# Output projection of a gated attention kernel over 448 instead of 512 rows: the last four heads' rows moved into padding rows, the rest as pairs of 64-row tiles

## The chip, the core and the metric

The kernel runs on one core of one Trainium2 chip. Its engines work side by side, each from its own list of instructions in order: TensorE (PE in the profile, its weight loads PEld), VectorE (DVE), ScalarE (ACT), GpSimd (POOL) and SyncE (SP), which here only issues DMAs. The time is the device time of one launch in microseconds (us). PE multiplies a stationary tile of up to 128 rows (the contraction) by 128 columns with a stream of up to 512 columns and adds into PSUM, which has 8 banks here of 128 x 512 f32.

## The reference

Two branches share the input x of 2048 tokens by 448 features and are mixed by a gate of one value per token.

```
g = sigmoid((x * gate_w).sum(-1))
a = A(x):  q, k, v = x @ wq, x @ wk, x @ wv         # 16 heads of 28
           4 segments of 512 tokens; in each, per head
             a_dot = softmax(q k^T / sqrt(28) + causal mask) v
             a_mem = phi(q) M / (phi(q) z + 1e-6)    # M, z: sums over earlier segments
             o = sigmoid(beta) * a_mem + (1 - sigmoid(beta)) * a_dot
           a = o @ wo                                # 448 x 448: the output projection
b = B(x):  an MLP over the token axis: layernorm, w1 (2048 x 1792), gelu, w2 (1792 x 2048)
out = g * a + (1 - g) * b
```

The change concerns `o @ wo`: for each of 16 tiles of 128 tokens, a contraction over the 448 rows (16 heads of 28).

## The kernel before

**Heads and padding.** Attention wants the heads at multiples of 32 rows. `qT` (128 rows, 4 head groups, 2048 tokens; L428 on, reused as `oT` for the attention's output) holds four heads in each group: head l at rows 32 l to 32 l + 27, and four padding rows behind it. So 448 rows of `o` lie in 4 x 128 = 512 rows. `wo_sb` (128 rows, 4 groups, 448 columns) holds wo in the same layout. `load_wo` brings it by four DMAs, and `pool_clears` sets it to zero beforehand with one memset on POOL, so that the padding rows count for nothing. `wo_tile(T)` makes one tile of 128 tokens: four full matmuls, one for each head group, into one PSUM bank, and then an evacuation `ag`, which may be on ACT or DVE, that applies the gate and adds the MLP's bias.

**Order.** `Sched` collects operations with what they read and write, and works out the waits. The order on every engine isn't worked out: it is written by name in the table `ORDER`, five lists, together with the PSUM bank that an operation takes (`wo12=7` takes bank 7). Banks 4 to 7 are shared by projections, attention, output projection and MLP; an operation that takes a bank waits for those that read its last content. SP issues its DMAs in the order of its list, and a DMA that has to wait for something keeps back those behind it.

**Names.** u is a matmul of the MLP's first layer, y of its second (`y9-3`: tile 9, fourth matmul); `ldw1_k` and `ldw2_k` load their weights into three slots, in turn, so that a load waits until the tiles that used the slot three loads ago are done. k, q and v with letters are the projections. `sc` are the scores, `exp` the exponentials on ACT, `pv` the product with v, `mem` the memory part, `mst` the memory's state. On DVE `ta` and `tm` transpose pv's and mem's results from PSUM, `eps`, `rec`, `oa`, `om` normalize, `o` on POOL adds the two, and `ot` transposes the sum back into `oT`; unit u has segment u // 4 and head group u % 4, so ot15 is the last. `fin` adds the MLP's part and `out` stores a tile. `gk`, `gq`: the last heads' rows of k and q go by DMA to DRAM (`spare_heads`) and back to the place where attention wants them. `tk` and `dtx` are DMA transposes.

**Tile shapes on PE.** Full matmuls have 128 rows and 128 columns. The scores use 28 of 32 rows, four heads side by side (L973). `pv` and `mst` use 32 columns, four side by side (L1011, L858). The projections have pairs of 64 rows (L711). `Sched.columns` turns a short run of full matmuls next to a `pv` or `mst` into four column tiles each (L286 instead of L284).

Of the kernel before, what the change touches and what calls it, by code (L numbers as in the profile page):

```python
# [7 lines left out]
BF16 = mybir.dt.bfloat16  # L8
# [3 lines left out]
S = 2048  # L12
# [62 lines left out]
class Sched:  # L75
# [13 lines left out]
    def op(self, eng, fn, reads=(), writes=(), name=None, dma=False, out=False, cost=100.0, prio=0.0, mode=None,  # L89
           nbytes=0, rel=0.0, port=False, take=None, use=(), alt=None, split=None):  # L90
# [24 lines left out]
        if dma:  # L115
            self._dma_uid += 1
            o.evspace = "dma_u%d" % self._dma_uid
            o.is_event = True
# [183 lines left out]
def pool_cost(n):  # L302
# [7 lines left out]
        warm fill0 fill1 fill2 trx1_0=4 trx1_1=5 trx0_0=6 fill3 gtr trx0_1=7 fill4 fill5 v03t v03s v03a v03b v03c  # L310
        k0a=45 v03d k0c k0b=67 q0a k0d q0b q0d q0c v67a=54 sc0_0 v67c k1a=67 k1c sc0_1 k1b=45 k1d q1a=67 sc0_2 q1c
        q1b=45 q1d sc0_3 u0-0=6 u1-0:2=7 u0-1:2 u1-2:2 pv0=4 u0-3 sc0_4 u1-4 u0-4 u1-5 btr=5 u2-0=4 u1-6 u0-5:2 u2-1:2
        u1-7 u3-0=5 u0-7 u3-1 sc1_0 u3-2:2 u2-3 u0-8:2 u2-4 u0-10 u1-8:2 u3-4 u1-10 sc1_1 u0-11 u1-11 u3-5 u1-12
        u0-12:2 u1-13 u0-14 u1-14 u0-15 u2-5 u1-15 u2-6:2 u3-6 u2-8 u3-7:2 sc1_2 u3-9 u5-0=6 u2-9 u3-10:2 u2-10:2 u5-1
        pv1=7 sc1_3 u5-2 u2-12 u5-3 u2-13 u4-0=7 u5-4 u4-1:5 u3-12 u4-6 u2-14:2 u4-7 u5-5 sc1_4 u4-8 u3-13 u4-9 u5-6
        u3-14:2 u5-7:2 u6-0=4 u5-9 u4-10:2 u6-1 u4-12:2 u6-2 u4-14 sc2_0 u7-0=5 u5-10 u4-15 u5-11 u7-1:2 u6-3:2 u7-3
        u5-12:2 u7-4 sc2_1 u7-5 u5-14 u7-6:3 pv2=7 u5-15 u6-5 u7-9 u6-6:3 u7-10 sc2_2 u6-9 mst0=7 u6-10:2 pv3=6 u7-11
        u6-12 u7-12 sc2_3 u7-13 u8-0:2=7 u7-14 u9-0=6 u6-13 u9-1:2 u6-14 u8-2 u7-15 u8-3 sc2_4 u6-15 u8-4 u9-3 u8-5
        u9-4 u8-6:2 u9-5 pv4=5 u9-6 sc3_0 u9-7 u8-8:2 u9-8 u8-10 mem4=4 u9-9 u8-11 u9-10:4 u8-12:2 u9-14:2 u8-14:2
        k2a=45 sc3_1 k2c k2b=67 k2d sc3_2 q2a=54 q2b=67 q2c q2d sc3_3 v96a=45 v96b=67 v96c v96d sc3_4 u11-0:4=4 mem6=5  # L320
        u10-0:3=7 u11-4 u10-3 pv6=6 u10-4 u11-5 pv5=5 sc4_0 u10-5:3 u13-0=5 u10-8 u11-6:2 u10-9 u13-1 mem5=6 u11-8
        u10-10 sc4_1 u10-11:2 u11-9 u10-13 u13-2 u10-14 u11-10 u13-3 u10-15 u11-11:3 u13-4 u11-14:2 u13-5 sc4_2
        u12-0:6=6 pv7=7 u12-6 u13-6 u12-7 sc4_3 mst1=4 u12-8 u13-7:2 mem7=7 u13-9 u12-9 u13-10 u12-10 sc4_4 u13-11
        u12-11 u13-12 u12-12:3 wo2=4 u12-15 wo3=7 u13-13:3 wo0~2=4 wo1=7 sc5_0 k3a=64 k3b=57 k3c k3d sc5_1 v14a=46
        pv8=5 v14c pv9=7 wo5=5 mem9=4 sc5_2 q3a=76 q3b=54 q3c q3d sc5_3 y0-0:5=7 y1-0:2=6 y0-5 y3-0:2=4 y1-2 y3-2:2
        mem8=5 y0-6 y1-3 y3-4 sc5_4 y3-5:2 y0-7 y3-7 y0-8:2 y1-4:2 y3-8:2 y0-10 sc6_0 y3-10 y0-11:2 y3-11 wo4=5 y1-6
        y3-12 y1-7 y0-13 sc6_1 y1-8:2 y3-13 y1-10:2 mem11=5 wo6=7 y1-12:2 y4-0=5 sc6_2 pv11=4 y4-1:2 y2-0=6 y4-3
        y2-1:2 y4-4 pv10=4 y4-5 sc6_3 y2-3 y4-6 y2-4 y4-7:2 mem10=7 y4-9 y5-0:2=4 y2-5:2 sc6_4 y2-7 y5-2 mst2=7 y2-8:2
        y5-3:3 y2-10 y4-10 y5-6 sc7_0 y2-11 y5-7 y2-12 y6-0=7 y5-8:3 y2-13 y6-1 y4-11 y6-2 y5-11 y4-12 sc7_1 y5-12
        y4-13 y6-3 pv12=6 y5-13 wo7=5 sc7_2 y6-4:4 y7-0:4=5 y6-8 mem12=6 y6-9 y7-4:4 mem13=4 y6-10 y7-8:2 sc7_3 pv13=6  # L330
        y6-11:3 wo9=4 y7-10 sc7_4 y7-11:2 mem14=6 y7-13 wo8=4 pv14=7 wo10=6 wo11=5 pv15=4 y8-0:2=7 y9-0:2=5 y8-2
        y9-2:3 mem15=6 y8-3 y9-5:2 y8-4:4 y9-7 y8-8:2 y9-8:2 y11-0=6 y10-0:2=4 y9-10 y11-1 y10-2 y8-10:2 y9-11 y11-2
        y8-12:2 y11-3 y10-3 y9-12:2 y11-4 y10-4 y11-5:2 y10-5 y11-7:2 y10-6:2 y11-9 y10-8 y11-10:2 y10-9:2 y11-12
        y10-11 y11-13 y10-12:2 wo12=7 wo14=6 wo13=4 y13-0=5 wo15=7 y15-0=6 y13-1 y15-1 y13-2:2 y15-2 y13-4:2 y14-0:4=4
        y15-3 y13-6:2 y12-0:2=7 y14-4:3 y12-2 y15-4 y13-8 y14-7 y15-5:2 y14-8 y13-9 y12-3 y14-9:3 y12-4 y13-10 y15-7
        y14-12 y12-5 y13-11 y15-8 y13-12 y15-9:2 y13-13 y12-6:4 y14-13 y15-11 y12-10 y15-12:2 y12-11:3 y15-0~2=5
# [3 lines left out]
        ldx2 ldwv1 ldwv2 xTcp0_10 xTcp0_00 cpv0 cpv1 cpv2 gt0 gt1 cpv3 gt2 cpk0_0 ek0_0 gt3 cpk0_3 ek0_1 cpk0_2 cpv4  # L340
        cpq0_1 gt4 cpq0_3 tb exp0_0=2 gt7 gt6 cpk1_0 exp0_1=3 cpk1_2 cpq1_3 exp0_2=4 cpq1_1 exp0_3=0 cpv5 gt5 eq1_0
# [42 lines left out]
        gq2_3 ldw2_0 ldwo0 gq2_1 gk2_0 tk1_2 gq2_2 tk2_1 ldwo1 gq2_h1 gk2_1 gq2_h2 gq2_h0 ldw2_1 gk2_h1 gk3_2 gk2_h0  # L384
        tk2_0 ldw2_2 gq3_3 tk2_3 gk3_3 gq3_2 gq3_1 tk2_2 gq3_0 gk3_0 gk3_1 ldw2_3 gq3_h2 gk3_h0 out0 out1 out3 gq3_h1
        gk3_h1 gq3_h0 out2 out5 ldw2_4 ldw2_5 ldw2_6 out4 out7 out6 ldw2_7 out9 out8 out11 out10 out13 out14 out15
        out12 out15~2
    """,
}

# [860 lines left out]
```

The softmax here doesn't subtract the row's maximum and nothing guards it: scores larger than these inputs give would overflow.

## Time and profile before

| what | us |
|---|---|
| median of 5 runs (lowest, highest) | 173.49 (172.94, 174.56) |
| the profiled execution, and its span | 174.56, 172.8 |
| PE busy in the span | 166.5 |
| DVE, ACT, POOL busy | 144.4, 127.0, 68.4 |
| last matmul before the end of the attention (pv15) ends at | 145.87 |
| last ot (ot14) starts at | 154.96 |
| last output DMA issued, landed | 170.86, 172.35 |

The span runs from the first to the last instruction; the time of the execution holds 1.76 us more. Matmuls overlap: [...]what it costs in a stream is the distance to the next start. Instructions that wait, and SP's issues, don't count as busy.

### The profile page before, as it was taken

To read this page: it belongs to the slowest core of one execution; us is meant where nothing else is said; L and a number is where in the kernel's file an instruction comes from. 1 tells how busy PE (TensorE), PEld (TensorE's weight loads), DVE (VectorE), ACT (ScalarE), POOL (GpSimd) and SP (SyncE) were. 2 spreads that over 40 slices of the span, in tenths; PEclk is the share of its full clock that TensorE was granted. 3 is DMA by queue.
4 is the path that set the end of the run, shared out by engine and by line. 5 is a ranking of instruction groups with operands and counts; after the bars stand their busy time and mean duration, and the time that the engine had idled before them with its cause. 6 is when DMAs were issued, how large, how long until landed. Compare 5 with 4: busy or idle time off the path is not lost.

```text
span 172.8 us, 4764 instructions
## 1 busy us (share of the span) xinstructions
PE 166.5 (96%) x1960; PEld 80.4 (47%) x1960; DVE 144.4 (84%) x324; ACT 127.0 (73%) x154; POOL 68.4 (40%) x98
## 2 busy tenths in 40 slices
PE   7996999999999999999999999999999999999994
PEld 2544334445445444445455435444554445555553
DVE  1975999969897999999999999996998999977115
ACT  2375999998999999998999999989667876001000
POOL 8040457441554203193351561047736856150000
PEclk9999999999999999999999999999999999999999
DMA  5998996528382955579237000732820089825203
GB/s 171 262 236 252 304 292 152 104 67 233 66 239 40 148 126 154 110 215 282 56 76 223 0 4 10 208 70 52 239 87 30 0 233 292 226 81 172 67 0 106
DMA packets 49733, 24.57 MB, mean 142 GB/s; under 512 B 14240, under 2 KB 49472, under 8 KB 49712
## 3 DMA queue, kind: packets, MB, share of 16 engines
q1 hardware_dynamic: 49024, 23.70, 53.8%
q10 hardware_dynamic: 688, 0.57, 1.1%
q8 instruction: 15, 0.25, 0.6%
q14 instruction: 6, 0.05, 0.1%
HBM read 18.76 MB, written 2.36 MB: 122 GB/s over the span
## 4 chain that ended last, share of the span: by engine, by line
PE 72%; DVE 9%; ACT 7%; SPq 5%; DMA 3%; issue 2%; ACTq 0%
PE t L284 36%; PE t L711 15%; PE t L286 11%; PE t L973 6%; PE t L1011 4%; ACT t L982 3%; DMA t<-in_A_x_dram 3%; DVE t L1093 2%; SPq L536 2%; DVE t L1095 2%; ACT t L1087 1%; DVE t L1100 1%; ACT t L1098 1%; DVE t L806 1%; ACT t L815 1%
## 5 line engine op out<-in xcount | busy, mean ns | idle before, releaser
L982 ACT ACTIVATE t<-t 128x2048 bf16<-128x2048 f32 x40 | 75.1, 1878 | 8.3 <-PE t L973 8.0
L284 PE MATMUL t<-t 128*128 128x448 bf16 (+3 forms) x411 | 79.1, 347 | 0.2 <-DVE t L1100 0.2
L985 POOL TENSOR_SCALAR_AFFINE_SELECT t<-t 128x512 bf16<-128x512 bf16 x64 | 42.4, 681 | 48.3 <-ACT t L982 47.8
L284 PEld LDWEIGHTS t<-t 128*128 128x128 bf16 x411 | 37.8, 98 | 37.2 <-issue 4.4
L711 PE MATMUL t<-t 64*128 64x512 bf16 (+1 forms) x308 | 35.4, 368 | 2.0 <-DMA t<-in_A_x_dram 1.5
L286 PE MATMUL t<-t 128*32 128x448 bf16 (+1 forms) x508 | 28.7, 354 | 0.0
L1042 POOL TENSOR_TENSOR t<-t 128x448 bf16<-128x448 f32 x12 | 15.6, 1302 | 23.6 <-DVE t L1038 6.8
L711 PEld LDWEIGHTS t<-t 64*128 64x128 bf16 x308 | 15.7, 94 | 18.9 <-PE t L711 3.2
L1118 DVE SCALAR_TENSOR_TENSOR t<-t 128x448 bf16<-128x448 f32 (+2 forms) x17 | 10.6, 644 | 9.3 <-PE t L284 8.6
L1067 ACT ACTIVATE t<-t 128x448 bf16<-128x448 f32 x10 | 7.2, 725 | 13.2 <-PE t L284 11.6
L286 PEld LDWEIGHTS t<-t 128*32 128x32 bf16 x508 | 12.3, 96 | 8.9 <-issue 1.9
L973 PE MATMUL t<-t 28*128 28x512 bf16 (+3 forms) x256 | 15.8, 301 | 0.3
L1048 DVE STREAM_TRANSPOSE t<-t 128x512 bf16<-128x512 bf16 x16 | 10.9, 692 | 1.1 <-POOL t L1042 1.1
L916 DVE BATCH_NORM_STATS2 t<-t 128x6 f32<-128x448 bf16 x16 | 9.3, 606 | 2.8 <-DMA t<-in_A_x_dram 2.8
L1011 PE MATMUL t<-t 128*32 128x512 bf16 (+3 forms) x256 | 11.5, 300 | 0.0
L1027 DVE STREAM_TRANSPOSE t<-t 128x512 f32<-128x512 f32 x16 | 11.1, 698 | 0.2
L973 PEld LDWEIGHTS t<-t 28*128 28x128 bf16 x256 | 4.5, 92 | 14.5 <-ACT t L982 7.1
L1025 DVE STREAM_TRANSPOSE t<-t 128x512 f32<-128x512 f32 x12 | 8.6, 713 | 2.3 <-PE t L284 1.7
L1095 DVE SCALAR_TENSOR_TENSOR t<-t 128x448 f32<-128x448 f32 x14 | 9.1, 646 | 1.0 <-ACT t L1090 0.9
L1100 DVE SCALAR_TENSOR_TENSOR t<-t 128x448 bf16<-128x448 f32 x14 | 8.9, 639 | 0.4 <-ACT t L1098 0.4
L1011 PEld LDWEIGHTS t<-t 128*32 128x32 bf16 x256 | 6.4, 96 | 5.9 <-issue 1.0
L795 DVE SCALAR_TENSOR_TENSOR t<-t 128x512 bf16<-128x512 bf16 x12 | 8.7, 727 | 0.0
(73 smaller groups left out, 162.9 us busy)
## 6 DMA issues: line engine op xcount, KB each, us to landing
t<-in_B_w_dram SPq DMA_DIRECT2D x7, 1024.0 KB, 6.3
t<-in_B_w_dram SPq DMA_DIRECT2D x8, 896.0 KB, 6.1
out_dram<-t SPq DMA_DIRECT2D x15, 112.0 KB, 1.8
t<-in_A_x_dram SPq DMA_DIRECT2D x3, 448.0 KB, 5.3
t<-in_A_wo_dram SPq DMA_DIRECT2D x4, 98.0 KB
t<-in_A_wk_dram SPq DMA_DIRECT2D x1, 336.0 KB, 4.4
t<-in_A_wq_dram SPq DMA_DIRECT2D x1, 336.0 KB, 4.8
spare_heads<-t SPq DMA_DIRECT2D x8, 32.0 KB
```

Of the source, the lines that this page charges most:

```text
L284: return e.matmul(out, w, x, skip_group_check=True, **kw)
L286: last = e.matmul(out[q : q + 32], w[:, q : q + 32], x, skip_group_check=True, **kw)
L711: last = e.matmul(bank(o["b"])[:, 0 : o["n"]], o["w"](r, c), o["x"](r, c), start=first, stop=end, skip_group_check=True)
L973: last = e.matmul(bank(hl)[:, c0 : c0 + w], kT[r, hg, s * 512 + j * 128 : s * 512 + j * 128 + 128], qT[r, hg, s * 512 + 128 * j : s * 512 ...
L982: op("ACT", lambda e: e.activation(pslot(g), ps[:, 0:4, :], ACT.Exp, scale=SCALE), reads=R_bank[0:4], writes=[g.res], take=g, name=f"exp{p ...
L985: op("POOL", lambda e, c0=c0: e.affine_select(pslot(g)[:, :, c0 : c0 + 128], pslot(g)[:, :, c0 : c0 + 128], pattern=[[0, 4], [1, 128]], co ...
L1011: last = e.matmul(bank(cb)[32 * hl : 32 * hl + 32, 128 * j : 512], vaug[:, 4 * s + j, 32 * h : 32 * h + 32], pslot(P_fill[u // 2][f])[:, h ...
L1027: dv(lambda e: e.transpose(t2[:, 0, :], bank(cb)[:, 0:512]), [bres(cb)], [R_tt[tb][0]], "ta", 630, use=(cb,))
L1042: op("POOL", lambda e: e.tensor_tensor(o3, n3[0], n3[1], op=ALU.add), reads=R_tt[tb], writes=[R_ob[tb]], name=f"o{u}", cost=1280, port=Tru ...
L1048: dv(lambda e: e.transpose(oT[:, hg, s * 512 : s * 512 + 512], o), [R_ob[tb]], qres(hg, s), "ot", 635)
L1095: op("DVE", lambda e: e.scalar_tensor_tensor(gg[:, q, :], gg[:, q, :], 1.0, vh[:, q, :], op0=ALU.add, op1=ALU.mult), reads=[R_gg[q], R_vh[ ...
L1100: op("DVE", lambda e: e.scalar_tensor_tensor(uT[:, ft, :], gg[:, q, :], 1.0, vh[:, q, :], op0=ALU.add, op1=ALU.mult), reads=[R_gg[q], R_vh ...
```

## The change

The contraction becomes 448 rows: three full matmuls of 128 rows and one half of 64.

- `load_wo` puts rows 336 to 383 of wo into the padding rows of groups 0 to 2 (12 rows each, `ldwo4` to `ldwo7`), and the other 64 rows (384 to 447) twice into group 3, in rows 0 to 63 and 64 to 127 (`ldwo8` to `ldwo15`). All 512 rows of `wo_sb` are written, and the clear is gone.
- `scatter(s)`, once for each segment of 512 tokens, moves the same rows of `oT`: two DMAs (`sd`) copy the first two heads of group 3, 56 rows, to DRAM (`spare_out`), once the segment's last ot is done; four (`sa`) bring 48 rows from there into the padding rows of groups 0 to 2; two (`sb`) bring the other 8 rows behind heads 3 and 4 of group 3; one (`sc…x`) copies those 64 rows to rows 0 to 63, for the segment's first 256 tokens.
- `wo_group(s)` makes four tiles with four banks: in each three full matmuls, and then two operations `woh`. Each is a pair of 64-row matmuls into two banks: rows 0 to 63 for tile t, rows 64 to 127 for tile t + 2.
- `wo_group` comes after the segment's fourth unit. Before, tile u - 4 came with unit u.
- DMAs of one kind share a semaphore (`space`).
- All five lists of `ORDER` are new. The PE list has 475 entries instead of 469, the SP list 155 instead of 107.

```diff
-           nbytes=0, rel=0.0, port=False, take=None, use=(), alt=None, split=None):
+           nbytes=0, rel=0.0, port=False, take=None, use=(), alt=None, split=None, space=None):
...
-            o.evspace = "dma_u%d" % self._dma_uid
+            o.evspace = "dma_" + space if space else "dma_u%d" % self._dma_uid
...
+    spare_o = nc.dram_tensor("spare_out", (56, S), BF16, kind="Internal").ap()
...
         for hl in range(4):
-            op("SP", lambda e, hl=hl: e.dma_start(wo_sb[32 * hl : 32 * hl + DH, :, :],
-                                                  WO.rearrange("(g l d) m -> l d g m", g=NHG, l=4)[hl]),
-               reads=[R_wv[0]], writes=[R_wo[hl]], name=f"ldwo{hl}", dma=True, cost=500, nbytes=126000)
+            ld(hl, hl, wo_sb[32 * hl : 32 * hl + DH, 0:3, :], WO.rearrange("(g l d) m -> l d g m", g=NHG, l=4)[hl, :, 0:3])
+            ld(4 + hl, 4 + hl, wo_sb[32 * hl + DH : 32 * hl + 32, 0:3, :],
+               WO[336:384].rearrange("(g l d) m -> l d g m", g=3, l=4)[hl])
+        for k, (row, w0, n) in enumerate(((64, 392, DH), (92, 384, 4), (96, 420, DH), (124, 388, 4))):
+            for h in range(2):
+                ld(8 + 2 * k + h, 8 + 2 * k + h, wo_sb[row - 64 * h : row - 64 * h + n, 3, :], WO[w0 : w0 + n])
...
-        op("POOL", lambda e: e.memset(wo_sb[:].bitcast(U32), 0), reads=R_xT[1], writes=R_wo, name="wo0",
-           cost=pool_cost(896))
...
+    def scatter(s):
+        ts = slice(s * 512, s * 512 + 512)
+        src = qres(3, s)
...
+        for k in range(2):
+            mv(spare_o[DH * k : DH * k + DH, ts], oT[32 * k : 32 * k + DH, 3, ts], src, [R_so[s][k]], f"sd{s}_{k}")
+        for i in range(4):
+            mv(oT[DH + i : 128 : 32, 0:3, ts], spare_o[0:48].rearrange("(g b i) t -> i b g t", g=3, b=4)[i, :, :, ts],
+               R_so[s] + [R_qT[g][s] for g in range(3)], [R_pad[s][i]], f"sa{s}_{i}")
+        for k in range(2):
+            mv(oT[92 + 32 * k : 96 + 32 * k, 3, ts], spare_o[48 + 4 * k : 52 + 4 * k, ts], src + R_so[s], [R_oB[s][k]], f"sb{s}_{k}")
+        half = slice(s * 512, s * 512 + 256)
+        mv(oT[0:64, 3, half], oT[64:128, 3, half], src + R_so[s] + R_oB[s], [R_oC[s]], f"sc{s}x")
+
+    def wo_group(s):
+        b = [Bank() for _ in range(4)]
+        for t in range(4):
+            wo_tile(4 * s + t, b[t])
+        for t in range(2):
+            T = 4 * s + t
+
+            def fn(e, t=t, T=T):
+                e.matmul(bank(b[t])[:, 0:D], oT[0:64, 3, T * 128 : T * 128 + 128], wo_sb[0:64, 3, :], start=False, stop=True,
+                         skip_group_check=True)
+                return e.matmul(bank(b[t + 2])[:, 0:D], oT[64:128, 3, T * 128 + 256 : T * 128 + 384], wo_sb[64:128, 3, :],
+                                start=False, stop=True, skip_group_check=True)
...
-            for hg in range(NHG):
+            for hg in range(3):
                 last = mm(e, bank(b)[:, 0:D], oT[:, hg, T * 128 : T * 128 + 128], wo_sb[:, hg, :], split,
-                          start=(hg == 0), stop=(hg == NHG - 1))
+                          start=(hg == 0), stop=False)
...
-        if u >= 4:
-            wo_tile(u - 4)
-    for T in range(12, 16):
-        wo_tile(T)
+        if u % 4 == 3:
+            scatter(u // 4)
+            wo_group(u // 4)
```

Of the new lists, the places around the output projection. PE:

```
    sc4_4 u13-11 wo0=6 wo2=7 woh0 u12-14 u13-12:2 u12-15 u13-14:2 wo3=6 wo1=7 woh1 sc5_0
    ...
    y1-5 sc6_0 y3-6:2 y0-12 y1-6 y0-13 wo4=4 y1-7 y3-8 wo6=5 sc6_1 woh4 y1-8:3 y3-9:2 y1-11:3 mem11=5
    y3-11 sc6_2 y3-12:2 wo5=4 pv11=6 wo7=7 woh5 sc6_3
    ...
    y7-12:2 y6-12:2 wo10=5 wo8=4 woh8 mem15=7 pv15=6 wo9=5 wo11=7 woh9 y8-0=4 y9-0=6
    ...
    y10-10:4 wo12=6 wo14=4 woh12 wo13=5 y13-0:2=7 y12-0=6 y13-2:2 wo15=4 y12-1 y13-4:2 woh13 y12-2:5
```

SP, and DVE near the end:

```
    gk2_3 sd0_0 sd0_1 gq2_3 gq2_0 gq2_1 tk1_3 gq2_2 sa0_3 sb0_1 gk2_0 ldwo7 sa0_1 sb0_0 ldwo15 gk2_h1 gq2_h1 tk1_2
    ldwo14 gq2_h0 gq2_h2 ldwo5 sa0_0 gk2_h0 ldwo4 sa0_2 sc0x ldwo8 tk2_1 ldw2_1 ldw2_0 ldw2_2 sd1_0 sd1_1
    ...
    sd2_1 gk3_h1 sd2_0 sb2_1 out2 ldw2_4 sa2_2 sb2_0 sa2_0 sa2_3 out5 out4 sa2_1 sc2x ldw2_5 ldw2_6 out7 out6
    sd3_1 sd3_0 sb3_1 sb3_0 sa3_3 sa3_1 sa3_2 sa3_0 sc3x ldw2_7 out11 out10 out8 out9

    tm15 ta15 eps15 rec15 oa15 om15 eps14 ot12 b2g3 ot15 rec14 oa14 om14 ot14 fin9 fin8 fin10 fin11 ag14 ag15
```

## The prediction, made before the changed kernel ran

> **What bounds the kernel now.** I read the page's busy shares first, then who TensorE (PE) waited for, then its timeline, then the chain of waits, and last the timelines of VectorE (DVE) and of SyncE's DMA queue (SP). Busy shares, page part 1:
>
> ```profile
> PE 166.5 (96%) x1960; PEld 80.4 (47%) x1960; DVE 144.4 (84%) x324; ACT 127.0 (73%) x154; POOL 68.4 (40%) x98
> ```
>
> A busy PE can still be a slow PE, so the waits of PE alone (us in total, times, longest):
>
> ```profile
> PE t L711 <- DMA t<-in_A_x_dram: 1.5, 1, 1.5
> PE t L640 <- PEq L1236: 0.8, 1, 0.8
> PE t L683 <- DMA t<-in_A_x_dram: 0.4, 1, 0.4
> PE t L843 <- DMA t<-in_gate_w_dram: 0.3, 1, 0.3
> PE t L284 <- DVE t L1100: 0.2, 1, 0.2
> ```
>
> Four of the five lie before 14.4 us; after that PE streams to the end. Its timeline (start, length, line, x instructions) gives the prices of what it streams:
>
> ```profile
> 74.42 2.84 PE L711 MATMUL t<-t 64*128 64x449 bf16 x28
> 77.19 0.40 PE L973 MATMUL t<-t 28*128 28x384 bf16 x8
> ...
> 92.80 5.09 PE L284 MATMUL t<-t 128*128 128x448 bf16 x26
> 97.82 0.39 PE L973 MATMUL t<-t 28*128 28x512 bf16 x4
> ...
> 115.47 2.44 PE L284 MATMUL t<-t 128*128 128x448 bf16 x12
> 117.84 0.40 PE L973 MATMUL t<-t 28*128 28x384 bf16 x8
> ```
>
> From one start to the next, 26 full matmuls take 97.82 - 92.80 = 5.02 us and 12 take 117.84 - 115.47 = 2.37. The 14 between them are 2.65, so one full 128x128 matmul of 448 columns costs 0.189 us, and 5.02 - 26 x 0.189 = 0.10 us is left over in each stretch: the price of going from full tiles to the row tiles of the scores. The 28 half-height matmuls of 449 columns are 14 pairs: (2.77 - 0.10) / 14 = 0.191 us for a pair. The chain that ended last closes with PE alone:
>
> ```profile
> 143.82 1.51 PE t L286 x32
> 145.33 0.54 PE t L1011 x16
> 145.87 24.59 PE t L284 x143
> 170.48 0.35 DVE t L1118
> ```
>
> So whatever shortens PE's stream shortens the kernel, if nothing makes PE wait. But DVE and POOL finish the last attention units only while PE works on y8 to y11. DVE's timeline (tm15, then ot15 and ot14; brackets: idle before, released by):
>
> ```profile
> 147.84 0.72 DVE L1025 STREAM_TRANSPOSE t<-t 128x512 f32<-128x512 f32 x1 [0.26 <-POOL t L1042]
> ...
> 153.87 0.71 DVE L1048 STREAM_TRANSPOSE t<-t 128x512 bf16<-128x512 bf16 x1 [0.68 <-POOL t L1042]
> 154.96 0.71 DVE L1048 STREAM_TRANSPOSE t<-t 128x512 bf16<-128x512 bf16 x1 [0.38 <-POOL t L1042]
> ```
>
> And SP, in order of issue:
>
> ```profile
> 25.31 4.63 SPq L772 DMA_DIRECT2D spare_heads<-t  x8
> ...
> 120.67 0.41 SPq L582 DMA_DIRECT2D t<-in_B_w_dram  x1
> ...
> 122.41 2.18 SPq L1122 DMA_DIRECT2D out_dram<-t  x3
> ```
>
> A small copy costs SP 0.3 to 0.6 us to issue, and a free output landed 1.8 us after its issue (page part 6).
>
> **What the Trainium skill says.** "TensorEngine Tiling (Array Packing)", Key Properties: changing the tiling mode drains TensorE, changing only the tile does not. The trace agrees: 0.10 us at each change. "TensorE: Matmul & The Clock Gate", Part 3: tiles in different row groups run side by side, starting about 4 ns apart. The trace agrees: a pair of half-height matmuls takes 0.191 us where one full matmul takes 0.189. "DMA: Bandwidth & Descriptors", Queues, rings and completion order: each DMA engine consumes a ring's descriptors in order. The landings here fit it: the output issued at 122.41 landed 5.30 us later, right after the weights issued at 120.67.
>
> **The change part by part, for PE.** Removed: the fourth matmul of 16 tiles, 16 x 0.189 = 3.02 us. Added: 8 pairs (woh) at 0.19 = 1.52. Bare gain 1.50 us. But a pair is a third tile shape amid full ones, and a change of shape costs 0.10. I laid both PE orders out by shape (full, 32-column split as `columns` sets it, 32-row scores, 64-row pairs) and counted: 86 changes before, 97 after. Only woh1, woh4 and woh5 touch a score and cost one extra change each; the other five cost two; the rest of the new order saves two: 3 + 10 - 2 = 11, at 0.097 (the leftover unrounded) 1.07 us. Eight fewer column-split tiles are worth 0.02. Net on PE: -3.02 + 1.52 + 1.07 - 0.02 = -0.45 us.
>
> **The other engines.** The clear of wo_sb (0.84 us on POOL) goes; POOL is 40% busy and nothing queued for it, so nothing. Two DVE and ACT evacuations trade places; by median step per kind, DVE's list is 137.5 us of work instead of 140.1: no gain while PE bounds, but some room. SP gets 48 more DMAs (107 entries become 155): 12 weight pieces and nine moves for each of four groups, at about 0.45 us 22 us of issue in a queue that now sits waiting for tens of us; its total is no bound, its order is. Before the stall at 14.4 us the queue keeps the same count of issues ahead of the transposing load of x, so that stall stays at 1.5 us.
>
> **The new waits.** In each group the copy out (sd) waits for the last head group's ot, two DMAs; the eight pad rows' copies (sa, sb) wait for their landing; sc waits for sb. Behind sd in SP's in-order queue stand gathers and weight loads. The trace has no such chain, so I build it from its parts: issue 0.4 and landing 1.8, two sb and four sa issues 6 x 0.4 = 2.4, landing 1.8: 6.4 us from the end of ot to padded rows; bounds 5 (faster issues at 0.3, landings of 1.5) and 11 (behind a weight load of 5 us).
> Groups 0 to 2, from the positions in both lists with the times of before: group 0 has wo_sb's last piece and its pads some 2 us before wo0; group 1 about 1 us; group 2's pads land behind ldw2_4, some 1 us before wo10, and ldw2_5 stands behind sc2x, with 1 us left before y10. gk3_h1 stands behind sd2_1, so it waits for ot11; about level with the score that needs it. I take 0.2 us for these four, between 0 and 1.5.
> Group 3: between the end of pv15 and wo12 PE now has wo9, wo11 and 56 matmuls of y8 to y11: 62 x 0.189 + 0.19 + 0.3 of changes = 12.2 us. Less the 6.4 of the chain, ot15 has to end within 5.8 us of pv15. By dependence alone it can: tm, ta, eps, rec, oa, om 3.0, POOL 1.3, ot 0.65, about 4.9. Before, it took 154.58 - 145.87 = 8.7, because DVE came late to tm15. In the new DVE order 2.3 us less work stands ahead of tm15, which puts ot15 at about 6.6 us after pv15, and wo12 0.8 us late. wo11 takes the PSUM bank that tm15 empties, and may stall first by the same lateness (DVE would then hold up PE once, not twice). I take 0.6 us, between 0 and 2.9.
> Sum: -0.45 + 0.2 + 0.6 = +0.35 us, on a span of 172.8. The profiled execution took 174.56, 1.76 of it outside the span, and the median of the five is 173.49, so 1.07 us below the profiled one; the difference carries over: 173.8.
>
> **The rivals.** (1) The forecast: gain of -0.45 spent on short waits, 173.8. For it: PE's list is that full, and each new chain is timed to within a microsecond. Chance 0.45; its own range 172.9 to 174.6.
> (2) The last chain is late (the other side): DVE reaches tm15 as late as before, ot15 ends 8.7 us after pv15, wo12 waits 8.7 + 6.4 - 12.2 = 2.9 us. -0.45 + 2.9 = +2.45: 175.9. It decides as soon as ot15 ends 7.1 us after pv15 (then 1.3 us of wait less 0.45 is slower by 0.87). For it: DVE is busy 8.0 to 9.7 of every 10 us from 60 to 150. Against: 2.3 us less work ahead. Partial lateness counts here too. Chance 0.27.
> (3) SP's order: an earlier wait (sd2_1 on ot11, sc2x ahead of ldw2_5) blocks a gather or weight load, and PE stalls in mid-run, bound 1.5 us and more if a DMA queues behind a 5 us load: -0.45 + 2 = 175.0. For it: landings behind a load took 5.3 instead of 1.8. Against: most loads have many us of slack. Chance 0.12.
> (4) Everything arrives in time, and the new order also loses the small pauses after 14.4 (starts 0.1 to 0.3 us later than the prices say, at 56.96, 62.47, 64.07 and 101.72 in the trace, some 0.7 us in all): -0.45 - 0.6: 172.4. Chance 0.16. That the pairs don't run side by side is excluded by 0.191.
>
> **How the numbers follow.** About 0.5% (0.87 us) is what can be told from no change. Faster by more needs (4) at its full size: 0.17. Slower takes (2), (3) and a little of the upper end of (1): 0.41. The rest, 0.42, within. The range 172.3 to 175.8 leaves out about 0.1 on each side: below, the best of (4); above, the full size of (2).
>
> **What would show it.** PE's total of waits after 14.4 us and where they stand; woh pairs at 0.19 with 0.10 on each side; the start of wo12 against the landing of the last sa3; the end of ot15 less the end of pv15 (5.8 is the point); tm15's start against wo11. Wrong would be: a gain above 0.9 us, which needs fewer changes of shape than I counted, or a stall at a weight load that I gave slack.

## The result, and the profile after

The changed kernel took 174.34 us (median of 43 runs, 173.36 to 175.73) beside 173.60 us of the kernel before (80 runs). The ratio is 1.0049, with a 95% interval of 1.0034 to 1.0064: some 0.85 us slower, just at the 0.5% that the prediction took as the least that can be told from no change. A second set, measured later with the experiments, gave 1.0024 (1.0001 to 1.0046). "After" and "before" are the two kernels below; "after again" and "before again" are second profiles of them.

The busy shares of after (page part 1):

```profile
PE 169.3 (97%) x1906; PEld 80.4 (46%) x1906; DVE 143.6 (83%) x317; ACT 129.1 (74%) x158; POOL 69.1 (40%) x100
```

TensorE (PE) has lost 54 instructions and is still busy for longer. Its waits of 0.2 us and more (us in total, times, longest) show no new one:

```profile
PE t L650 <- PEq L1283: 0.8, 1, 0.8
PE t L693 <- DMA t<-in_A_x_dram: 0.6, 1, 0.6
PE t L983 <- ACT t L907: 0.2, 1, 0.2
```

The last one ends at the first scores (18.18 us), the other two lie ahead of them. After again has two more, of 0.8 and 0.3 us, ahead of its first scores too. There is no wait for a moved row (L1069) and none for a load of weights. The new pairs, in TensorE's timeline (start, length, engine, line, x instructions), lie as they were priced:

```profile
94.17 1.50 PE L284 MATMUL t<-t 128*128 128x448 bf16 x7
95.59 0.36 PE L1090 MATMUL t<-t 64*128 64x448 bf16 x1
95.60 0.36 PE L1092 MATMUL t<-t 64*128 64x448 bf16 x1
95.89 2.62 PE L284 MATMUL t<-t 128*128 128x448 bf16 x12
```

From one start to the next: 7 full matmuls and the way into the pair take 95.59 - 94.17 = 1.42 us, which is 7 x 0.189 + 0.10; the two halves of the pair start 0.01 us apart (3 to 4 ns in the unrounded records); the pair and the way out take 0.30, which is 0.19 + 0.10.

So the arithmetic holds and no wait shows, and the kernel is slower. To find where, I measured from the first scores to the start of the last matmul. What lies ahead of the first scores changes from one execution to the next (15.9 to 18.2 us in the 14 profiles, of both kernels and all variants), and it hid everything else at first. From the first scores on, two profiles of the kernel before differ by 0.08 us, two of after by 0.13. The difference between the kernels there, 0.60 to 0.81 us, is of the size of the 0.74 between their median times; whether late starts are equally frequent in both was not measured.

| from the first scores to the last matmul, us | before | before again | after | after again |
|---|---|---|---|---|
| measured | 152.44 | 152.52 | 153.12 | 153.25 |

I then priced both orders matmul by matmul, with the prices of the prediction and 0.097 us for each change of tile shape. The priced lists are 149.57 us before and 149.14 after: -0.43. What is measured above the price I call a pause of TensorE, however short; a part of it is the same in both (the first stretch, waits for its own matmuls). The scores come in eight blocks of five; they mark the stretches (profiles before again and after again):

| stretch | pauses before, us | pauses after, us |
|---|---|---|
| first scores to the third of block 1 | 0.97 | 1.03 |
| to the last of block 1 | 0.11 | 0.80 |
| to the third of block 2 | 0.06 | 0.06 |
| to the second of block 3 | 0.70 | 0.36 |
| to the last of block 4 | 0.65 | 0.71 |
| to the last of block 5 | 0.19 | 0.75 |
| to the last of block 7 | 0.25 | 0.19 |
| to the last matmul | 0.02 | 0.21 |
| sum | 2.95 | 4.11 |

The pauses grew by 1.16 us, the list shrank by 0.43: 1.16 - 0.43 = 0.73, the difference measured. The rows that grew add up to 1.56 us. The largest of them (0.69) lies between the third and the last scores of block 1, far ahead of the first projection tile, in work that the change doesn't touch except by its order. The second (0.56) lies between the last scores of blocks 4 and 5, behind the first projection tiles. The first place, in before again and then in after again (same start of the scores, 16.67 and 16.65):

```profile
37.29 0.40 PE L973 MATMUL t<-t 28*128 28x256 bf16 x8
37.61 1.77 PE L286 MATMUL t<-t 128*32 128x448 bf16 x32
39.21 0.72 PE L1011 MATMUL t<-t 128*32 128x512 bf16 x16
39.86 0.39 PE L973 MATMUL t<-t 28*128 28x512 bf16 x4
```

```profile
37.51 0.40 PE L983 MATMUL t<-t 28*128 28x256 bf16 x8
37.84 1.61 PE L286 MATMUL t<-t 128*32 128x448 bf16 x24
39.45 0.73 PE L1021 MATMUL t<-t 128*32 128x512 bf16 x16
39.99 1.13 PE L286 MATMUL t<-t 128*32 128x448 bf16 x20
41.06 0.39 PE L983 MATMUL t<-t 28*128 28x512 bf16 x4
```

Four column-split instructions make one tile. Before, 8 tiles run from 37.61 to 39.21: 1.60 us, 0.20 a tile. After, 6 tiles take 39.45 - 37.84 = 1.61, 0.27 a tile: two pauses (0.28 and 0.16 us), at a tile that takes a PSUM bank not yet emptied and at the attention output behind it. A third one (0.29) stands at the next tile that takes a bank. A timeline that joins such instructions to one group doesn't print these pauses, and the table of waits, which lists 0.2 us and more of the matmul alone, doesn't either: the wait is taken by the weight load.

The weight loads' timeline of after again names what ended five of the new pauses (brackets: idle before, released by). They stand ahead of two tiles of the MLP's first layer, a projection tile (wo3), the second part of a v projection (v14c) and a part of a q projection (q3b):

```profile
38.32 0.12 PEld L286 LDWEIGHTS t<-t 128*32 128x32 bf16 x8 [0.38 <-DVE t L1141]
41.86 0.11 PEld L284 LDWEIGHTS t<-t 128*128 128x128 bf16 x2 [0.38 <-DVE t L1037]
95.80 0.11 PEld L284 LDWEIGHTS t<-t 128*128 128x128 bf16 x2 [0.44 <-ACT t L1115]
102.12 0.11 PEld L721 LDWEIGHTS t<-t 64*128 64x128 bf16 x4 [0.51 <-PE t L721]
105.72 0.12 PEld L721 LDWEIGHTS t<-t 64*128 64x128 bf16 x4 [0.51 <-DVE t L1035]
```

A weight load is often idle for longer than TensorE is; TensorE's own pauses at these places are 0.28, 0.29, 0.16, 0.24 and 0.18 us. Four of them are banks that VectorE (DVE) or ScalarE (ACT) had not emptied. The one of 0.24 is TensorE's own: v14c waits for v14a, right ahead of it in the new order; in the old one pv8 stood between them. For the 0.16 at the attention output the profile names nothing.

### The profile page after: what moved, and what is told of

It reads as the page before. It is cut to its first block, busy times and chain, and to the rows that moved or that the text cites. A ratio compares the mean times of both kernels' runs of the same rounds, so it can differ in the third digit from the quotient of the medians.

```text
span 173.9 us, 4699 instructions
## 1 busy us (share of the span) xinstructions
PE 169.3 (97%) x1906; PEld 80.4 (46%) x1906; DVE 143.6 (83%) x317; ACT 129.1 (74%) x158; POOL 69.1 (40%) x100
## 4 chain that ended last, share of the span: by engine, by line
PE 70%; DVE 16%; ACT 8%; DMA 2%; issue 1%; POOL 1%; DVEq 0%; ACTq 0%
PE t L284 33%; PE t L721 16%; PE t L286 9%; PE t L983 5%; PE t L1021 4%; DVE t L1143 2%; ACT t L992 2%; DMA t<-in_A_x_dram 2%; DVE t L1148 2%; DVE t L1037 2%; DVE t L1141 2%; ACT t L1135 1%; PE t L1090 1%; ACT t L801 1%; DVE t L805 1%
## 5 line engine op out<-in xcount | busy, mean ns | idle before, releaser
L284 PE MATMUL t<-t 128*128 128x448 bf16 (+3 forms) x413 | 80.4, 347 | 0.1
L995 POOL TENSOR_SCALAR_AFFINE_SELECT t<-t 128x512 bf16<-128x512 bf16 x64 | 43.0, 688 | 50.0 <-ACT t L992 49.2
L721 PE MATMUL t<-t 64*128 64x512 bf16 (+1 forms) x308 | 36.6, 379 | 0.5
L286 PE MATMUL t<-t 128*32 128x448 bf16 (+1 forms) x436 | 25.7, 355 | 0.1
L1115 ACT ACTIVATE t<-t 128x448 bf16<-128x448 f32 x11 | 7.7, 722 | 17.8 <-PE t L1092 17.8
L286 PEld LDWEIGHTS t<-t 128*32 128x32 bf16 x436 | 10.5, 96 | 8.1 <-issue 2.6
L840 ACT ACTIVATE t<-t 128x448 bf16<-128x448 f32 x12 | 6.5, 545 | 4.2 <-PE t L721 4.1
L1135 ACT ACTIVATE t<-t 128x448 f32<-128x448 f32 x14 | 8.6, 636 | 1.2 <-DVE t L906 1.1
L1021 PEld LDWEIGHTS t<-t 128*32 128x32 bf16 x256 | 6.7, 96 | 5.2 <-issue 0.8
```

The lines of the kernel that those rows point to most:

```text
L284: return e.matmul(out, w, x, skip_group_check=True, **kw)
L286: last = e.matmul(out[q : q + 32], w[:, q : q + 32], x, skip_group_check=True, **kw)
L721: last = e.matmul(bank(o["b"])[:, 0 : o["n"]], o["w"](r, c), o["x"](r, c), start=first, stop=end, skip_group_check=True)
L995: op("POOL", lambda e, c0=c0: e.affine_select(pslot(g)[:, :, c0 : c0 + 128], pslot(g)[:, :, c0 : c0 + 128], pattern=[[0, 4], [1, 128]], co ...
L1021: last = e.matmul(bank(cb)[32 * hl : 32 * hl + 32, 128 * j : 512], vaug[:, 4 * s + j, 32 * h : 32 * h + 32], pslot(P_fill[u // 2][f])[:, h ...
```

## The experiments

Each kernel is timed against the kernel before, which ran beside it on the same chip. "Since the scores" is the measure above, from each one's profile.

### Is it the moves, the start, or the order?

**e2, no moves.** After, without the 36 moves. What the moves carry of the last four heads is missing from the output.

```diff
-            scatter(u // 4)
-        ... sd0_0 sd0_1 gq2_3 gq2_0 gq2_1 tk1_3 gq2_2 sa0_3 sb0_1 gk2_0
+        ... gq2_3 gq2_0 gq2_1 tk1_3 gq2_2 gk2_0
```

> The changed kernel without the 36 DMAs of scatter; it leaves the moving of the last four heads' rows out, so the padding rows hold what the projections left there. Every other instruction is the same. Theory: TensorE never waited for a move, so the time stays within 0.2 us of the changed kernel, 0.4 to 0.5% above before. Rival: the DMAs cost SP's queue and their landings cost TensorE, and the time falls by 0.6 us or more, to that of before.

Measured: 174.05 us, ratio 1.0040 (1.0015 to 1.0065); 153.14 since the scores, beside 153.12. No cost of the moves shows: the difference is 0.02 us.

**e1, the start.** After, with the first tiles of TensorE in the sequence that the kernel before has.

```diff
-        warm fill0 fill1 trx1_0=4 trx1_1=5 trx0_0=6 trx0_1=7 gtr fill2 fill3 fill4 fill5
+        warm fill0 fill1 fill2 trx1_0=4 trx1_1=5 trx0_0=6 fill3 gtr trx0_1=7 fill4 fill5
```

> The changed kernel with one edit: at the start TensorE does its warming matmuls in the order of before (three fills ahead of the first transposes, one more between them) instead of two ahead and the rest behind. Theory (the new order costs the time, not the moves): the first transposes start 56 ns apart as before, not 107, v03's pairs 0.19 us apart, not 0.37; the first scores start at 17.8 instead of 18.2 us; the time is 0.3 to 0.4 us below the changed kernel, some 0.3% above before. Rival (the moves by DMA and their waits cost the time): the scores start no earlier or the gain is lost later, the time stays 0.5% above before.

Measured: 174.06 us, ratio 1.0014 (0.9989 to 1.0039); the scores came at 16.25 us. But they came at 16.39 and 16.49 in e2 and e4 too, which have the start of after. The slow start of the first profile was that execution's, not the order's: the theory fell. The ratio alone doesn't decide it, since its interval overlaps those of e2 and e4. Since the scores it is 153.52 us, 0.40 more than after, though the list from there on is the same; where that lies is said below.

**e4, the new order alone.** After, with the old projection over 512 rows (four matmuls for each tile, no pairs, no moves) in the new order of all engines.

```diff
-        for t in range(2):
+        for t in range(0):
...
-            for hg in range(3):
+            for hg in range(4):
...
-                          start=(hg == 0), stop=False)
+                          start=(hg == 0), stop=(hg == 3))
...
-            scatter(u // 4)
```

> The new order of all engines, but the output projection as before: four full matmuls in each tile, no pairs, no moves (the wo rows loaded into the padding rows are multiplied with what lies in oT's padding rows, which before were zeros). Theory: TensorE has 16 x 0.189 us more and 8 x 0.19 and 13 changes of shape at 0.097 less than the changed kernel, +0.24 us; with the new order's slow start and its pauses about 1.1 us (0.6%) above before. Rival (the moves cost it): at the time of before, within 0.2 us.

Measured: 174.30 us, ratio 1.0045 (1.0021 to 1.0068); 153.32 since the scores. With the change undone and only the order kept, the loss is all there (+0.88 over the 152.44 of before), and the change itself, in that order, is worth 0.20 us (153.32 less 153.12). By its own list e4 is 0.34 us longer than after: 16 matmuls, less 8 pairs and 12 changes of shape. So part of the change's gain arrives. "Order" here means all five lists, and with them which engine does a step: 15 evacuations went from VectorE to ScalarE, 11 the other way.

**e5, the old first half.** After, with every engine's order up to the second scores of block 3 as before, and from there as after.

```diff
-        exp1_1=6 gsq0 ek0_3 gsq1 exp1_2=2 gth1 gth0 ek1_0
+        exp1_1=6 eq1_2 gsq0 gsq1 ek0_3 exp1_2=2 gth0 exp1_3=3 eq1_3 gth1
...
```

> The changed kernel with the order of before on all engines until TensorE's k2a (about 66 us), and the new order of what is left from there; the move of rows and the pairs stay. Theory: TensorE reaches sc3_1 at 67.6 as before instead of 68.3, and the whole time comes within 0.3 us of before (ratio 0.999 to 1.002), because the net of pairs and shape changes is -0.45 us and the later part of the new order has some 0.5 us of pauses. Rival: no better than the changed kernel, 1.005.

Measured: 174.19 us, ratio 1.0035 (1.0010 to 1.0059); 153.24 since the scores. In total it is no better than after, as the rival had it. Up to the seam 49.82 since the scores (before 49.83, after 50.12), so the first half's part of the loss went, as expected. From there 103.42 (before 102.61, after 103.00): the second half kept its own and lost some 0.4 more at the seam. Both halves of the order have pauses of their own.

### Is the measure sound?

**before again, after again.** The two kernels once more, unchanged.

> The kernel before, once more, for its profile. Theory (the start of a run varies, what follows does not): the first scores come at 16.2 to 16.8 us or near 18, whichever start this run has, but from them to the start of the last matmul it is 152.44 us again, within 0.05. Rival (the whole run varies from one execution to the next, so that differences of half a microsecond in one profile mean nothing): the stretch differs from 152.44 by 0.2 us or more.

> The changed kernel, once more. Theory: from its first scores to its last matmul 153.12 us again, within 0.05, whatever the start; the pauses of TensorE stand at the same places with the same lengths. Rival (noise): they move. The ratio is 1.003 to 1.007 against the kernel before.

Measured: 152.52 (0.03 more than the bound that was set) and 153.25 (0.08 more). The pauses stand at the same places in both profiles of a kernel. What differs lies at one place: between the third and fourth scores of block 2, where after again lost 0.21 more than after. There TensorE ends a run of 64 very small matmuls; see the last section. In e1, with the same list from the first scores on, this place cost 0.49 us more than in after. That is beyond the 0.2 that the rival named, at this one place. Without the stretch between these two scores the four profiles of that list (after, after again, e1, e2) lie between 150.35 and 150.46 us, the two of before at 149.63 and 149.71. So totals are compared below with this place in view; without it e4 has 150.63, e6 150.14, e8 149.98, e9 150.30 and e10 149.94.

### Are the pauses each their own, or does another engine set the pace?

**e6, the last pairs together.** After, with the last four tiles in banks 0 to 3, so that both pairs stand side by side, with two changes of shape fewer.

```diff
-        y8-12:2 ... wo12=6 wo14=4 woh12 wo13=5 y13-0:2=7 y12-0=6 y13-2:2 wo15=4 y12-1 y13-4:2 woh13
+        y8-12:2 ... wo12=0 wo14=2 wo13=1 wo15=3 woh12 woh13 y13-0:2=7 y12-0=6 y13-2:2 y12-1 y13-4:2
```

> The last group's four output tiles in four other banks, so that both of its pairs of 64-row tiles stand side by side: two changes of tile shape fewer, nothing else. Theory (a change of shape costs 0.097 us, no pad row is late): from the first scores to the last matmul 152.93 us, 0.19 less than after; ratio about 1.003 to 1.004. Rival (the last moves are nearly late, so the earlier second pair waits): no gain, and a wait of TensorE at the first of the four tiles or at the pairs.

Measured: 173.66 us, ratio 1.0007 (0.9980 to 1.0034). From the last scores to the last matmul 31.96 us instead of 32.17: -0.21, as priced. Since the scores it is 153.15 all the same, because the place after the small matmuls cost 0.32 us more in this profile than in after. The interval of its ratio overlaps that of after again, so the times alone don't show the gain. The two pairs lie 0.20 us apart in its timeline:

```profile
157.99 0.36 PE L1090 MATMUL t<-t 64*128 64x448 bf16 x1
157.99 0.36 PE L1092 MATMUL t<-t 64*128 64x448 bf16 x1
158.19 0.35 PE L1090 MATMUL t<-t 64*128 64x448 bf16 x1
```

**e7, the pauses mended.** e6, with five pauses bought off by exchange of neighbours in TensorE's list.

```diff
-        sc1_2 u3-7 u4-0=7 u3-8:2 u4-1 u3-10 pv1=6 u2-12:2 u4-2:2 u3-11 sc1_3 u4-4 u5-0=6 ...
+        sc1_2 u3-7:3 u4-0=7 u4-1 u3-10 u2-12:2 u4-2 pv1=6 u4-3 u3-11 sc1_3 u4-4 u3-12:2 u2-14:2 u4-5 u5-0=6 ...
-        q2a=54 q2b=67 q2c q2d        q3a=75 q3b=64 q3c q3d
+        q2a=54 q2c q2b=67 q2d        q3a=75 q3c q3b=64 q3d
```

> As e6, and five of TensorE's pauses taken out of the order by exchange of neighbours: the tile that takes bank 7 after the first MLP tile, the second attention output and the tile after it come 0.2 to 0.7 us later (pauses of 0.285, 0.16 and 0.29 us in after), and the q projections of two blocks run as first pair, third, second, fourth (0.25 and 0.17). Theory (what the change lost is the sum of such pauses, each at its own place): from the first scores to the last matmul 0.735 + 0.25 + 0.17 = 1.16 us less than e6, 151.8, less than the 152.44 of before; ratio 0.995 to 0.998. Rival (VectorE or ScalarE sets the pace and the pauses only show it): new pauses take their place within some 10 us, and the stretch stays within 0.3 us of e6.

Measured: 175.13 us, ratio 1.0084 (1.0057 to 1.0111); 153.96 since the scores, 0.81 more than e6. The theory fell. At the last scores of block 1 e7 is 0.69 us ahead of e6, as it should be; at the third of block 2 it is 0.30 behind. And each exchange of projections cost more than the pause it took out: the two stretches grew by 0.29 and 0.37 us, most of the 0.81, so the rival's bound of 0.3 missed as well. In the timeline, the q block of e6 and then of e7:

```profile
69.52 3.38 PE L721 MATMUL t<-t 64*128 64x512 bf16 x28
```

```profile
69.70 3.67 PE L720 MATMUL t<-t 64*128 64x512 bf16 x28
```

That part was my own mistake: in a projection the parts c and d wait for a and b (`project` appends that dependence), so a part right behind its own first one makes TensorE wait for its own matmul. The waits of the weight loads count four more such places, first in e6 and then in e7:

```profile
PEld t L721 <- PE t L721: 3.2, 7, 0.6
```

```profile
PEld t L720 <- PE t L720: 5.4, 11, 0.6
```

Where one falls, the matmul starts 0.44 us after the one before it instead of 0.22.

**e8, ScalarE ahead.** e6, with two exchanges in ScalarE's list.

```diff
-        exp1_1=6 gsq0 ek0_3 gsq1 exp1_2=2 gth1 gth0 ek1_0 exp1_3=3
+        exp1_1=6 ek0_3 gsq0 gsq1 exp1_2=2 gth1 ek1_0 gth0 exp1_3=3
```

> As e6, with two exchanges in ScalarE's list only: an exponential of the keys moved ahead of the first MLP tile's square, for which ScalarE stands idle 1.1 us in after, and another moved ahead of a tanh for which it stands idle 0.4 us. From 41 to 111 us ScalarE is never idle for more than 0.15 us in after, while the kernel before leaves it gaps there. Theory (ScalarE paces TensorE from 26 to 111 us; what the new order lost there is ScalarE's idle time ahead of that stretch): the pauses of TensorE at the second attention output and ahead of the fourth score of block 2 go (0.16 and about 0.3), from the first scores to the last matmul 152.6 to 152.8 instead of 153.15. Rival (VectorE paces it): 153.0 to 153.2, unchanged.

Measured: 173.81 us, ratio 1.0038 (1.0017 to 1.0060); 152.67 since the scores. ScalarE's timeline, in after again and then in e8 (e6 has the same times since the scores as after again here):

```profile
36.91 0.63 ACT L1135 ACTIVATE t<-t 128x448 f32<-128x448 f32 x1 [1.11 <-PE t L284]
37.45 0.62 ACT L801 ACTIVATE t<-t 128x512 bf16<-128x512 bf16 x1
```

```profile
35.59 0.62 ACT L802 ACTIVATE t<-t 128x512 bf16<-128x512 bf16 x1
36.81 1.16 ACT L1136 ACTIVATE t<-t 128x448 f32<-128x448 f32 x2 [0.59 <-DVE t L907]
```

The exponential (L801, in e8 L802) moved into the idle time, and the second square behind it comes 0.52 us earlier since the scores. What empties the second tile's bank on VectorE then comes 0.24 us earlier (21.74 instead of 21.98 us since the scores), and from there on VectorE's whole list does: its steps up to 46 us since the scores are 0.22 to 0.25 us earlier. At the third scores of block 2 TensorE is 0.25 us ahead. The rest of the 0.48 between e6 and e8 is the place after the small matmuls (0.32 less in this profile), of which 0.09 came back behind it. Beside after, where that place cost as little as in e8, e8 is 0.45 us shorter: 0.21 by the pairs, as in e6, and 0.25 by this. So the number fell into the theory's range, half of it by luck. The times don't show the gain: the interval of the ratio overlaps those of after and of e6.

**e9, both.** e8, with the first mend of e7.

> As e8, with the first mend of e7 as well (the three MLP and attention tiles after the fourth score of block 1 taken 0.2 to 0.7 us later in TensorE's list), without e7's exchange of the q projections, each of which put two pairs right behind the pair that they wait for. Theory (ScalarE paces): with ScalarE 0.9 us ahead, at least half of the 0.74 us that e7 won there and gave back by 53 us is kept: 152.1 to 152.5, about the 152.44 of before or less. Rival (VectorE paces): the pauses come back by 53 us as in e7: 153.0 to 153.3.

Measured: 174.26 us, ratio 1.0052 (1.0031 to 1.0073); 153.11 since the scores. TensorE is 0.53 us ahead of e8 at the last scores of block 1, 0.32 behind at the third of block 2, as in e7. Here the profile shows who took it back. VectorE and GpSimd (POOL), first in e8 and then in e9 (e9 started 1.39 us later):

```profile
46.78 0.68 DVE L831 SCALAR_TENSOR_TENSOR t<-t 128x512 bf16<-128x512 bf16 x1
```

```profile
46.85 4.80 POOL L996 TENSOR_SCALAR_AFFINE_SELECT t<-t 128x512 bf16<-128x512 bf16 x6 [2.94 <-ACT t L993]
```

```profile
48.17 1.12 DVE L832 SCALAR_TENSOR_TENSOR t<-t 128x512 bf16<-128x512 bf16 x1
```

```profile
47.83 4.10 POOL L997 TENSOR_SCALAR_AFFINE_SELECT t<-t 128x512 bf16<-128x512 bf16 x5 [2.53 <-ACT t L994]
```

In e8 the step of VectorE starts 0.07 us ahead of GpSimd's masks and takes 0.68 us. In e9 the scores, their exponential and so the masks come earlier, GpSimd starts 0.34 us ahead of VectorE, and the same step takes 1.12: 0.44 more. From there the delay can be followed: the argument of the fourth MLP tile's tanh (garg3) ends 0.44 us later, ScalarE stands idle for it, and its tanh starts 0.44 us later than in e8 (34.51 and 34.07 us since the scores). In e9's timeline of ScalarE:

```profile
52.44 0.58 ACT L1148 ACTIVATE t<-t 128x448 f32<-128x448 f32 x1 [0.87 <-DVE t L1145]
```

Behind it come ScalarE's next exponential (0.44 later) and the square of the sixth tile (0.44), and then all 44 steps of VectorE up to 60 us since the scores, each 0.43 to 0.45 us later than in e8. TensorE is 0.44 behind at the fourth scores of block 2. e7 against e6 shows the same step with 1.12 us and the same tanh 0.43 later. The Trainium skill, "SBUF — State Buffer", section "SBUF: two separate sides", states that VectorE and GpSimd share a port pair as an exclusive lock for a whole instruction, which a VectorE operation with two SBUF inputs needs against a GpSimd operation that reads SBUF. The profiles agree: VectorE's step took 0.44 us more when it started second, and in e8, where GpSimd's first mask started second, that mask took 1.11 us, where most masks take 0.63.

**e3, no pairs.** After without the eight pairs: the last 64 rows are left out of the product.

```diff
-        for t in range(2):
+        for t in range(0):
...
-                          start=(hg == 0), stop=False)
+                          start=(hg == 0), stop=(hg == 2))
```

> After without the eight pairs of 64-row tiles: the last 64 rows of the projection are left out of the output (all else, the moves too, is done). Theory (a pair and its changes of shape sit on TensorE's path at full price): from the first scores to the last matmul less by 8 x 0.19 + 13 x 0.097 = 2.8 us, 150.3 to 150.7. Rival (ScalarE or VectorE paces the middle, so that what is taken out there is given back as pauses): the four pairs of groups 0 and 1 give back part of their 1.2 us, and the stretch is 150.9 to 151.6.

Measured: one run of 174.76 us, with a late start (17.56); 152.88 since the scores, 0.37 less than after again, where some 2.7 us of TensorE's list are gone (8 pairs at 0.19, and 12 changes of shape, one fewer than expected: without the pairs `columns` splits 19 more operations). Both expectations missed. TensorE's timeline shows the two largest places where it was given back:

```profile
96.69 1.31 PE L284 MATMUL t<-t 128*128 128x448 bf16 x6 [0.40 <-ACT t L1115]
...
157.60 4.70 PE L284 MATMUL t<-t 128*128 128x448 bf16 x24 [1.06 <-DMA t<-spare_out]
```

At 96.69 the third tile waits for ScalarE to empty its bank, 0.40 us longer than in after. At 157.60 the last group's first tile waits for the moved rows, a pause of 1.22 in all. With 0.23, 0.39 and 0.16 at three more places that is 2.40 us. Of the 1.2 us that the four pairs of groups 0 and 1 are worth, 1.02 came back (0.40, 0.23, 0.39); most of the rest is the last group's wait for its rows, not another engine's pace.

**e10, the scores first.** e8, with one exchange at the pause ahead of the third tile of the projection.

```diff
-        u13-14:2 wo3=6 wo1=7 woh1 sc5_0 k3a=54
+        u13-14:2 sc5_0 wo3=6 wo1=7 woh1 k3a=54
```

> As e8, with one exchange more in TensorE's list: the first scores of block 5 ahead of the projection tiles wo3 and wo1 and their pair, instead of behind them, so that wo3 comes 0.3 us later in the list than the bank it takes is emptied (a pause of 0.16 us in after, e6 and e8). The number of changes of shape stays. Theory (a pause that ScalarE's lateness doesn't cause can be bought off for good): from the first scores to the last matmul 152.67 - 0.16 = 152.5, level with the kernel before (152.44 to 152.52), ratio 0.999 to 1.002. Rival (ScalarE's full list behind it takes it back, as with e9's mend): 152.65 to 152.8, unchanged.

Measured: 175.21 us (7 runs), ratio 1.0083 (1.0052 to 1.0113); 153.10 since the scores, after a late start in the profile (18.24 us). From the last scores of block 4 to those of block 5 it takes 18.65 us, e8 18.60: the pause of 0.16 went, and new ones of 0.10, 0.09 and 0.11 came within 4 us. The rest of the distance from e8 lies at the place after the small matmuls. The rival was right.

### Who sets the pace

Busy time in two windows of 35 us, before again and then after again (columns: window, length, then busy us and instructions of PE, its weight loads, DVE, ACT, POOL; clock; DMA):

```profile
41.00:76.00 35.00, 34.32 (x440) 16.10 (x440) 31.94 (x68) 34.47 (x41) 13.83 (x19) 1.00 0.58 132
76.00:111.00 35.00, 34.85 (x485) 17.02 (x484) 33.74 (x71) 33.70 (x47) 12.76 (x19) 1.00 0.42 109
```

```profile
41.00:76.00 35.00, 34.72 (x432) 16.15 (x430) 33.90 (x66) 34.50 (x40) 11.98 (x17) 1.00 0.67 154
76.00:111.00 35.00, 34.56 (x442) 16.28 (x438) 32.87 (x69) 34.62 (x48) 16.92 (x22) 1.00 0.44 109
```

Three engines are full at once. ScalarE, 74% over the span, is busy 34.5 and 34.6 of 35 us after; VectorE 33.9 and 32.9. The kernel before stands close to it: ScalarE 34.5 and 33.7, VectorE 31.9 and 33.7. In that state the pauses of TensorE that were bought off came back within some 10 us (e7, e9, e10), and so did most of the work of groups 0 and 1 that was taken off TensorE alone (e3). Of the 0.34 us of the change itself 0.20 stayed (e4). What brought ScalarE and VectorE forward stayed (e8, one profile). In the stretch from 14 to 97 us since the scores, VectorE's steps that lasted over 0.2 us longer than their kind usually does (its lower quartile in these profiles) add up to 1.10 us before (3 of them) and 2.36 after (6). These 1.26 us are of the size of the 1.16 us of new pauses. That they cause all of them was not tried, and the sum doesn't follow the pauses one for one: in e8 it is 2.57, though e8 has 0.25 us of pauses less. That one such step delays both engines and then TensorE by its full 0.44 us is seen in e9 against e8. To put pv8 back between v14a and v14c, for the 0.24 us that TensorE there waits for itself, was not tried either.

No version beats the kernel before. The nearest are e6 in time (1.0007, 0.9980 to 1.0034) and e8 since the scores (152.67 against 152.44 and 152.52).

## Why the prediction was right and wrong

It said 173.8 us, within 0.5%, with 0.41 for slower; it came to 174.34, at that edge. The direction of the sum was right, and its second half had the wrong cause: 0.8 us of waits for moved rows, of which none came, stood in the sum where 1.16 us of other pauses came. That the total lay near is luck.

- **PE's list, -0.45 us.** Right: -0.43 by the full pricing, pairs at 0.19, each change of shape at 0.10, and e6 took out two changes for 0.21. But it was priced as if TensorE's list were the only one. In the new order the change alone is worth 0.20 us (after against e4), of 0.34 by the list.
- **The new waits of groups 0 to 2, +0.2.** Wrong: no wait there; e2 without any move is 0.02 us off.
- **Group 3, +0.6.** Wrong, though the margin was small. The last moved rows in after, VectorE's, SyncE's and TensorE's timelines:

```profile
149.33 0.71 DVE L1058 STREAM_TRANSPOSE t<-t 128x512 bf16<-128x512 bf16 x1
...
152.78 0.71 DVE L1058 STREAM_TRANSPOSE t<-t 128x512 bf16<-128x512 bf16 x1 [1.25 <-POOL t L1052]
```

```profile
150.07 0.76 SPq L1069 DMA_DIRECT2D spare_out<-t  x2
151.92 3.77 SPq L1069 DMA_DIRECT2D t<-spare_out  x6
```

```profile
147.04 11.90 PE L284 MATMUL t<-t 128*128 128x448 bf16 x62
158.88 0.36 PE L1090 MATMUL t<-t 64*128 64x448 bf16 x1
```

  ot15 (149.33) ended 4.5 us after pv15, sooner than the 6.6 expected (by its own figures, 8.7 less 2.3, it should have said 6.4) and inside the point of 5.8. But the four copies into the pads of the other head groups wait for ot14 as well (152.78 to 153.5), which my chain left out: they were issued from 153.52 on, the last at 155.19. wo12 is the sixth matmul ahead of 158.88, at about 157.65, and it found its rows. In e3 the last copy was issued at 155.55 and released wo12 at 157.60, 2.05 us later; by that, after had about 0.4 us to spare. Two errors of the chain, one each way, and a wait of nothing. wo11 didn't wait for tm15 either.
- **The other engines: "no gain while PE bounds, but some room".** This is the step that failed. I summed VectorE's list (2.6 us shorter; its busy time came out 0.8 shorter), took it that two evacuations trade places, and read ScalarE's 73% as room. By the lists 26 change places and ScalarE has four more. Its busy time is 2.1 us longer after, and over the windows above it had next to none to give, in the kernel before too. The waits that came stand mostly at PSUM banks that VectorE and ScalarE empty, from the third scores of block 1 on (0.28, 0.29, 0.18 and 0.16 us); 0.24 is a wait of TensorE for itself, and for 0.16 no cause is named.
- **Rival 4** took it that the new order would lose the small pauses of the old one. It lost 0.34 us of them between blocks 2 and 3, and brought some 1.5 of its own.
- **Rivals 2 and 3** didn't occur: no late last chain, no blocked load. With less of TensorE's own work the last chain would be late (e3).
- **The start.** The stall of 1.5 us at the transposing load was one execution's; before again had 0.2 and after none, where the prediction had it stay. From the first scores on, where it doesn't count, the difference is there.

## What to carry to other kernels

Before a change that shortens one engine's list by half a microsecond is priced, read the busy time of all engines in windows of some 30 us, not over the span: where a second and a third engine are as full as here (ScalarE 34.5 of 35 us, VectorE 33.9), a gain on the list that was shortened can come back as short pauses at the buffers they empty. A change that makes a new order of all engines has to be compared with its own order without the change; here the order cost 0.88 us and the change brought about 0.20. Pauses below 0.3 us didn't show in TensorE's own list of waits: price the list and subtract, and then ask the weight loads what they waited for.

## What the runs showed of the hardware that was not expected

- One VectorE step on two bf16 inputs took 0.68 us when it started ahead of GpSimd's mask, and 1.12 when GpSimd started first (e8, e9; the same in e7). An earlier score can so make VectorE later.
- A dependence of TensorE on its own matmul just before costs about 0.22 us (0.24 at v14c in after; e7: four more such places, and two stretches longer by 0.29 and 0.37 us although pauses of 0.25 and 0.17 went).
- After 64 matmuls of 32 columns TensorE stood still for up to half a microsecond (e1 0.49 more than after, e10 0.47) for nothing that the profile shows, differently in each execution. In e10 (the matmuls, and then the tiles behind them):

```profile
55.83 0.57 PE L869 MATMUL t<-t 128*32 128x32 bf16 x51
56.23 0.56 PE L286 MATMUL t<-t 128*32 128x448 bf16 x7
56.95 0.36 PE L286 MATMUL t<-t 128*32 128x448 bf16 x1 [0.17 <-issue]
```

- TensorE's first matmuls ran at two paces. The 16 transposes of x took 1.89 us in after and 1.07 in after again, the same program. The trace's record of the granted clock, 1.00, begins at 9.98 us in after and at 3.71 in after again; for the time ahead of it the trace has none. In after the projections' pairs of 449 columns start 0.37 us apart up to there, in after again 0.19. The three profiles whose record begins after 9 us (after 9.98, e9 9.47, e10 10.18) have their first scores at 18.18, 17.93 and 18.24 us. What sets the moment isn't shown.

```profile
4.11 1.89 PE L693 MATMUL t<-t 128*128 128x128 bf16 x16 [0.56 <-DMA t<-in_A_x_dram]
```

```profile
4.16 1.07 PE L693 MATMUL t<-t 128*128 128x128 bf16 x16 [0.61 <-DMA t<-in_A_x_dram]
```
